# A fused retention and bilinear feed-forward kernel: the opening's four steps in another order, with loads, casts, clears and one PSUM place moved

## The chip, the cores and the metric

The kernel runs on one core of one Trainium2 chip. The metric is the device time of one execution in microseconds; 335.1 us is the median of four runs of the kernel before (334.6 to 335.91). The profile is of one execution, the one that took 335.91 us.

In the profile, PE is TensorE (PEld its weight loads), DVE is VectorE, ACT is ScalarE, POOL is GpSimd and SP is SyncE, which here only issues DMAs. A trailing q, as in SPq or POOLq, is that engine's queue, where DMAs are issued.

## What is computed

A retention layer (attention with a decay in place of the softmax) and a bilinear feed-forward layer on its output, with 8 batches, 8 heads, 576 positions, a head width of 64, a model width of 512 and a feed-forward width of 1536:

```python
scores = scale * np.matmul(q, k.transpose(0, 1, 3, 2))
gamma = 1.0 - 2.0 ** (-5.0 - np.arange(H))
Dmat = np.where(rel >= 0, gamma[:, None, None] ** rel, 0.0)   # rel = row - column
attn = np.matmul(scores * Dmat, v)
x = attn.transpose(0, 2, 1, 3).reshape(B * S, H * D)          # 4608 x 512
out = ((x @ w_a) * (x @ w_b)) @ w_out                         # 4608 x 512
```

Inputs and output are fp32; the kernel multiplies in bf16 and sums in fp32.

## The kernel before, in words

**Retention without the full matrix.** The decay is split into a factor for the key, put on V (tables `vs`), and a factor for the query, put on the result (tables `qs`). Rows are taken in blocks. Within a block the kernel makes scores, masks the upper triangle, and multiplies by V; what earlier rows contribute comes from a state, the sum of outer products of K and V over those rows.

**The opening (lines 143 to 413 and 836 to 895).** The first 512 rows of batch 0 are done in four steps, `STEPS = [(0, 0), (1, 0), (0, 1), (1, 1)]`: step i is (n, hh), the 256 rows from 256 n and the heads from 4 hh. So steps 0 and 1 hold the first four heads, steps 2 and 3 the last four, and steps 1 and 3 need the sum over the rows of steps 0 and 2. For each step there are

- three loads of 256 KB each, Q, K and V (`load_step`, L154, on SP's queue, in an order written out by hand),
- casts of Q and K to bf16 on an engine named in the call (`cast_step`, L315: DVE, POOL or ACT), and V times its decay in two halves `kp` (`values_step`, L319),
- `transpose_step`: four PE transposes (L328) into one PSUM buffer, and a copy to SBUF (L330) on an engine named in the call,
- `score_step`: 16 small matmuls (L343) into the scores' PSUM tile of two banks (pool `ps_sc`, one buffer), and one masked product on DVE (L351) into `sT`, with `mask_s` that POOL makes at the start (L180 to L182),
- `state_step`: 16 or 32 matmuls (L371) of K and V, and two ACT copies (L380) of the result into the diagonal blocks of `state_after`, whose other blocks must be zero (the clear at L262, with that of `two_states`),
- `output_step`: matmuls from the state (L395) and from `sT` and V (L404) into a PSUM tile `o` of two banks (pool `ps_step`, one buffer), and a product with the table `qs` on DVE (L411) into `x`, the feed-forward input. The tables `qs` of the opening are four ACT instructions (`make_qs`, L224) that need an index cast by DVE (L220).

The order of all of these on each engine is the order of the calls at L841 to L895; nothing reorders it. Before, scores and states run in the order 0, 2, 1, 3 and 0, 1, 2, 3, and outputs in the order 0, 1, 2, 3. Between them stand calls `warm(count, n)` (L836): matmuls of a tile of ones whose result nobody reads, which fill PE while it would wait.

**Weights.** `load_w` (L266, L268) and `load_wo` (L271) issue the weight DMAs from POOL's queue, so they start where POOL's program has come to: the columns of the first three of twelve feed-forward tiles of `w_a` and `w_b` among the opening's steps, the others at its end. One later DMA on SP's queue, `gate` (L901), reads from the loaded `w_out`, so that SP's next loads start only when that has landed.

**Feed-forward.** `ffn_begin(F)` (L754) for F in 0, 1, 2 does the first two of the four contractions (`c` 0 and 1, the first four heads) of three tiles of `x @ w_a`, before the others' input exists. `ffn_block` then does, per block of 512 or 256 rows, the other matmuls with `w_a` (L772), with `w_b` (L787), the product of the two (L792), and `w_out` (L807). All three share the PSUM pool `ps_ffn` of four buffers with the transposes, the states and the warm matmuls. The rest of the retention is fed in between these matmuls at due times of a list (`todo`), in units of matmuls. Of these, the prediction speaks of the fifth and sixth 128-row parts of the old form (`one_by_one`, with DVE's cast at L428 and ACT's at L426) and of the POOL casts for later pairs (L555).

Of the kernel before, what the change touches and what calls it, by code (L numbers as in the profile page):

```python
# [10 lines left out]
FP32 = mybir.dt.float32  # L11
# [7 lines left out]
def kernel(  # L19
# [139 lines left out]

    STEPS = [(0, 0), (1, 0), (0, 1), (1, 1)]  # L160
    Q, K, V = 0, 1, 2
    for i, which in ((0, Q), (0, K), (2, K), (2, Q), (1, Q), (0, V),
                     (1, K), (1, V), (3, K), (3, Q), (2, V), (3, V)):
        load_step(*STEPS[i], which)


# [33 lines left out]

    ones = const.tile([128, 512], BF16)
    nc.vector.memset(ones, 1.0)  # L202
    lgp = const.tile([128, HP], FP32)
    for c in range(HP):
        nc.vector.memset(lgp[0:64, c:c + 1], math.log(gammas[2 * c]))
        nc.vector.memset(lgp[64:128, c:c + 1], math.log(gammas[2 * c + 1]))
    biasq = const.tile([128, 1], FP32)
    nc.vector.memset(biasq, math.log(scale))
    idxp_f = const.tile([128, 6], FP32)
    nc.vector.tensor_copy(idxp_f, idxp_i)  # L210
    nc.vector.tensor_scalar_add(idxp_f[64:128, 4:5], idxp_f[64:128, 4:5],
                                -float(S))
    vs = const.tile([128, H, 6], FP32)
    for h in range(H):
        nc.scalar.activation(vs[:, h, :], idxp_f, AF.Exp,
# [7 lines left out]
    def make_qs(c, s0, s1):  # L223
        nc.scalar.activation(qs[:, c, s0:s1], idx_f[:, s0:s1], AF.Exp,  # L224
                             bias=biasq[:, 0:1], scale=lgp[:, c:c + 1])
# [33 lines left out]
    states = [two_states[:, i] for i in (0, 1)]  # L259
    state_after = const.tile([128, 2, 2, HP, 128], BF16)  # L260
    for t in (state_after, two_states):
        nc.vector.memset(t, 0.0)  # L262

    def load_w(f0, f1, which="ab"):
        if "a" in which:
            nc.gpsimd.dma_start(wa_sb[:, :, f0:f1], wa_r[:, :, f0:f1])  # L266
        if "b" in which:
            nc.gpsimd.dma_start(wb_sb[:, :, f0:f1], wb_r[:, :, f0:f1])  # L268
# [45 lines left out]
    def cast_step(i, w, on):  # L314
        COPY[on](by_parity(natural[STEPS[i]][0][:, w]), given(i, w))  # L315

    def values_step(i, kp, on):
        n, hh = STEPS[i]
        on.tensor_tensor(  # L319
            by_parity(natural[n, hh][1])[:, :, kp], given(i, 2)[:, :, kp],  # L320
            vs[:, 4 * hh:4 * hh + 4, 2 * n + kp].unsqueeze(2)
            .to_broadcast([128, 4, D]), op=ALU.mult)

    def transpose_step(i, w, on):
        qkb, qkT = natural[STEPS[i]][0], transposed[STEPS[i]]
        tp = ps_ffn.tile([128, 4, 128], BF16, tag="ab", name="tp")
        for c in range(4):
            nc.tensor.transpose(tp[:, c, :], qkb[:, w, c * 128:c * 128 + 128],  # L328
                                identity)
        COPY[on](qkT[:, w], tp.rearrange("p c x -> p (c x)"))  # L330
# [5 lines left out]
    def score_step(i):  # L336
        key = STEPS[i]
        sc = ps_sc.tile([128, 2, 2, 2, 128], FP32, tag="sc", name="sc0")
        for j in (0, 1):
            for kp in (0, 1):  # L340
                for r, a in QUADS:
                    k0 = kp * 256 + j * 128 + a * 64
                    nc.tensor.matmul(  # L343
                        sc[half(a), r, j, kp],
                        transposed[key][half(r), 1, k0:k0 + 64],
                        queries(key, half(r), j, a),
                        start=(j == 0 and kp == 0), stop=True,
                        skip_group_check=True)
        sT = st_pool.tile([128, 2, 2, 2, 128], BF16, tag="sT", name="sT0")
        scored[key] = sT  # L350
        nc.vector.tensor_tensor(  # L351
            sT.rearrange("p r j k s -> p (r j) (k s)"),
            sc.rearrange("p r j k s -> p (r j) (k s)"),
            mask_s.rearrange("p k q s -> p (k q s)").unsqueeze(1)
            .to_broadcast([128, 4, 256]), op=ALU.mult)

    def state_step(i, behinds):

        n, hh = STEPS[i]
        kv = ps_ffn.tile([128, 2, 2, 64], FP32, tag="ab", name="kv0")  # L360
        fresh = {0, 1}
        for behind in behinds:
            parts = [(0, slice(0, 128))] if n else []
            parts.append((n, slice(0, 128) if behind else half(0)))
            for m, rows in parts:
                qkb, vb = natural[m, hh]
                for j in (0, 1):
                    for kp in (0, 1):
                        for r in (0, 1):
                            e0 = kp * 256 + (2 * j + r) * 64  # L370
                            nc.tensor.matmul(  # L371
                                kv[half(r), behind, j, :],
                                qkb[rows, 1, e0:e0 + 64],
                                vb[rows, e0:e0 + 64],
                                start=r in fresh, stop=True,
                                skip_group_check=True)
                            fresh.discard(r)
        which = slice(behinds[0], behinds[-1] + 1)
        for r in (0, 1):
            nc.scalar.copy(  # L380
                state_after[half(r), n, which, 2 * hh:2 * hh + 2, half(r)],
                kv[half(r), which])

    def output_step(i):
        n, hh = STEPS[i]
        vb = natural[n, hh][1]
        sT = scored.pop((n, hh))
        o = ps_o[0].tile([128, 2, 512], FP32, tag="o", name="o0")
        for a in (0, 1):
            if (n, a) == (0, 0):  # L390
                continue
            st = state_after[:, 0, 0] if (n, a) == (0, 1) else (
                state_after[:, n - 1 + a, 1 - a])
            for j in (0, 1):
                nc.tensor.matmul(o[:, a, 128 * j:128 * j + 128],  # L395
                                 st[:, 2 * hh + j, :],
                                 queries((n, hh), slice(0, 128), j, a),
                                 start=(j == 0), stop=True,
                                 skip_group_check=True)
        for j in (0, 1):  # L400
            for kp in (0, 1):
                for a, r in QUADS:
                    e0 = kp * 256 + (2 * j + r) * 64
                    nc.tensor.matmul(  # L404
                        o[half(r), a, 128 * j:128 * j + 128],
                        vb[half(a), e0:e0 + 64],
                        sT[half(a), r, j, kp],
                        start=((n, a, j, kp) == (0, 0, 0, 0)), stop=True,
                        skip_group_check=True)
        cs = slice(2 * hh, 2 * hh + 2)  # L410
        nc.vector.tensor_tensor(  # L411
            x_of(256 * n, 256)[:, cs].rearrange("p j (a s) -> p a j s", a=2),
            o[:, :, 0:256].rearrange("p a (j s) -> p a j s", j=2),
            qs[:, cs, 256 * n:256 * n + 256]
            .rearrange("p j (a s) -> p a j s", a=2), op=ALU.mult)
# [416 lines left out]
    def warm(count, n):  # L832

        w = ps_ffn.tile([128, 512], FP32, tag="ab", name="w")
        for _ in range(count):
            nc.tensor.matmul(w[:, 0:n], ones[:, 0:128], ones[:, 0:n],  # L836
                             start=True, stop=True)
# [1 line left out]
    W1, W2 = 128 * WCOLS[0], 128 * (WCOLS[0] + WCOLS[1])  # L839
    vector, pool_ = nc.vector, nc.gpsimd  # L840
    warm(8, 512)  # L841
    for c in range(HP):
        make_qs(c, 0, 512)
    for i in range(4):
        place_step(i)
    cast_step(0, Q, "dve")
    cast_step(0, K, "dve")
    transpose_step(0, Q, "dve")
    cast_step(2, K, "pool")
    transpose_step(0, K, "act")  # L850
    warm(4, 256)
    score_step(0)
    transpose_step(2, K, "act")
    warm(4, 256)
    cast_step(1, Q, "act")
    cast_step(2, Q, "pool")
    transpose_step(2, Q, "act")
    warm(4, 256)
    transpose_step(1, Q, "dve")
    values_step(0, 0, pool_)  # L860
    values_step(0, 1, vector)
    warm(2, 256)
    score_step(2)
    cast_step(1, K, "act")
    state_step(0, (0, 1))
    warm(4, 256)
    transpose_step(1, K, "act")
    load_w(0, W1, "a")
    values_step(1, 0, vector)
    warm(3, 256)  # L870
    output_step(0)
    values_step(1, 1, pool_)
    load_w(0, W1, "b")
    score_step(1)
    cast_step(3, K, "act")
    state_step(1, (0,))
    transpose_step(3, K, "act")
    cast_step(3, Q, "pool")
    warm(4, 256)
    transpose_step(3, Q, "act")  # L880
    values_step(2, 0, vector)
    values_step(2, 1, pool_)
    output_step(1)
    state_step(2, (0, 1))
    score_step(3)
    values_step(3, 1, pool_)
    warm(4, 256)
    output_step(2)
    values_step(3, 0, pool_)
    load_w(W1, W2)  # L890
    state_step(3, (0,))
    for F in range(3):
        ffn_begin(F)
    output_step(3)
    warm(3, 256)  # L895
    load_w(W2, DFF)
    for i in (0, 1, 2):
        load_wo(i)
# [100 lines left out]
```

## Time and profile before

| | |
|---|---|
| median of four runs | 335.1 us |
| lowest, highest | 334.6, 335.91 us |
| the profiled execution's own time | 335.91 us |
| its span, first to last instruction | 334.2 us |
| PE busy | 324.9 us, 97% |
| DVE, ACT, POOL busy | 166.8, 128.1, 113.6 us |
| HBM read, written | 37.75 MB, 9.44 MB |
| first matmul of `ffn_block` (L772) | 20.88 us |

The page gives the busy time of each engine, the span in 40 slices of 8.4 us (the tenths of each slice that an engine was busy, and the clock granted to TensorE), and groups of instructions by line with what ended the idle time ahead of them. The timeline lists instructions in order of time: start, length, engine, line, operation, output and inputs, count, and in brackets the idle time before it and what ended that. A row with a count is several instructions of one kind. Starts and lengths can overlap the row before on the same engine a little. The list of waits names the waiting line, its releaser, the total in us, how often, and the longest.

### The profile page before, as it was taken

Reading aid. Unit: us, or ns where it says so; the run is one execution under the profiler, and the core shown is the slowest. Engines: PE = TensorE matmul, PEld = TensorE weight load, DVE = VectorE, ACT = ScalarE, POOL = GpSimd, SP = SyncE. Lnnn points to the kernel's source line nnn. Section 1 sums busy time; section 2 is a strip of 40 time slices with the busy share of each in tenths; the row PEclk is TensorE's granted clock in tenths of the full one; section 3 lists DMA queues with packets and bytes.
Section 4 is the critical chain, followed back from the end, with each engine's and each line's share of the span. In section 5 each row is a group of like instructions: output and inputs, shape, how many; then the busy total and the mean of one; then the engine's idle time right before and its main releaser. Section 6 shows DMA issues by size and latency. Waiting matters only on the chain.

```text
span 334.2 us, 8646 instructions
## 1 busy us (share of the span) xinstructions
PE 324.9 (97%) x3616; PEld 167.6 (50%) x3616; DVE 166.8 (50%) x305; ACT 128.1 (38%) x270; POOL 113.6 (34%) x146
## 2 busy tenths in 40 slices
PE   6999998999999999999999999999999999999996
PEld 2744445857744454545454545454545454444443
DVE  6746337465746465476237623753475347413321
ACT  6734842443624343253225232523342335213321
POOL 4690028760547467267035602470240000000000
PEclk9999999999999999999999999999999999999999
DMA  7999999999999999997599449954970420020002
GB/s 209 233 170 205 208 207 208 230 198 185 179 207 236 216 213 237 191 216 121 148 213 202 66 141 190 212 93 129 198 116 3 125 67 0 3 94 31 2 31 94
DMA packets 146151, 50.37 MB, mean 151 GB/s; under 512 B 130624, under 2 KB 141632, under 8 KB 146112
## 3 DMA queue, kind: packets, MB, share of 16 engines
q1 hardware_dynamic: 141360, 45.10, 66.4%
q0 software_dynamic: 4752, 4.72, 8.9%
q8 instruction: 28, 0.46, 0.6%
q14 instruction: 11, 0.09, 0.1%
HBM read 37.75 MB, written 9.44 MB: 141 GB/s over the span
## 4 chain that ended last, share of the span: by engine, by line
PE 93%; DVE 2%; DMA 2%; ACT 1%; issue 1%; SPq 0%; POOL 0%; ACTq 0%; DVEq 0%; POOLq 0%
PE pa L772 28%; PE pb L787 28%; PE po L807 27%; DMA kf<-in_k_dram 2%; PE o L692 2%; PE o L705 1%; PE sc L666 1%; PE kv L615 1%; PE w L836 1%; PE kv L371 1%; PE tp L328 1%; PE o L404 0%; PE pa L754 0%; DVE xT L532 0%; DVE sT L498 0%
## 5 line engine op out<-in xcount | busy, mean ns | idle before, releaser
L792 DVE TENSOR_TENSOR hT<-ha,pb 128x512 bf16<-128x512 bf16 (+1 forms) x120 | 75.8, 633 | 97.9 <-PE pb L787 85.4
L780 ACT CAST ha<-pa 128x512 bf16<-128x512 f32 (+1 forms) x120 | 64.7, 542 | 123.4 <-PE pa L772 122.7
L787 PE MATMUL pb<-xT,wb_sb 128*128 128x512 bf16 (+1 forms) x480 | 111.8, 358 | 0.1
L772 PE MATMUL pa<-xT,wa_sb 128*128 128x512 bf16 (+1 forms) x474 | 110.3, 358 | 1.1 <-DVE xT L532 0.6
L807 PE MATMUL po<-wo_sb,hT 128*128 128x512 bf16 (+1 forms) x444 | 97.3, 374 | 0.0
L787 PEld LDWEIGHTS <-wb_sb 128*128 128x128 bf16 x480 | 46.7, 98 | 47.3 <-issue 1.1
L772 PEld LDWEIGHTS <-wa_sb 128*128 128x128 bf16 x474 | 45.3, 98 | 46.9 <-issue 2.4
L807 PEld LDWEIGHTS <-hT 128*128 128x128 bf16 x444 | 42.4, 98 | 47.0
L555 POOL CAST qkb<-qf 64x1024 bf16<-64x1024 f32 x15 | 15.4, 1030 | 85.4 <-DMA qf<-in_q_dram 78.0
L818 DVE COPY osb<-po 128x512 f32<-128x512 f32 (+1 forms) x18 | 12.2, 676 | 44.7 <-PE po L807 44.7
L560 POOL TENSOR_TENSOR vb<-vf,vs 128x1024 bf16<-128x1024 f32 x15 | 28.5, 1901 | 8.1 <-DMA vf<-in_v_dram 3.4
L816 ACT COPY osb<-po 128x512 f32<-128x512 f32 (+1 forms) x19 | 10.9, 574 | 45.3 <-PE po L807 45.3
L714 DVE TENSOR_TENSOR xT<-o,qs 128x512 bf16<-128x512 f32 x30 | 19.6, 681 | 5.3 <-PE o L705 5.3
L634 DVE TENSOR_TENSOR sums<-kv,sums 128x256 f32<-128x256 f32 x47 | 19.8, 422 | 4.6 <-PE kv L615 3.1
L675 DVE TENSOR_TENSOR sT<-sc,mask 128x512 bf16<-128x512 f32 x30 | 19.7, 679 | 0.0
L559 POOL CAST qkb<-qf 64x512 bf16<-64x512 f32 x30 | 17.7, 617 | 1.9 <-DMA qf<-in_q_dram 1.3
L559 POOL CAST qkb<-kf 64x512 bf16<-64x512 f32 x30 | 17.6, 614 | 0.9
L555 POOL CAST qkb<-kf 64x1024 bf16<-64x1024 f32 x15 | 15.5, 1033 | 7.0 <-DMA kf<-in_k_dram 6.7
L646 ACT CAST states<-sums 64x512 bf16<-64x512 f32 (+1 forms) x30 | 17.2, 574 | 0.5
L836 PE MATMUL w<-ones 128*128 128x256 bf16 (+1 forms) x40 | 8.4, 340 | 1.5 <-DVE ones L202 1.5
L431 POOL TENSOR_TENSOR vb<-vf,vs 128x512 bf16<-128x512 f32 x2 | 2.1, 1057 | 22.1 <-DMA vf<-in_v_dram 22.1
L224 ACT ACTIVATE qs<-qs,biasq,lgp 128x384 f32<-128x384 f32 (+1 forms) x12 | 8.0, 734 | 2.4 <-DVE qs L247 2.4
(103 smaller groups left out, 159.2 us busy)
## 6 DMA issues: line engine op xcount, KB each, us to landing
qf<-in_q_dram SPq DMA_DIRECT2D x32, 256.0 KB, 4.5
kf<-in_k_dram SPq DMA_DIRECT2D x32, 256.0 KB, 5.2
vf<-in_v_dram SPq DMA_DIRECT2D x32, 256.0 KB, 5.3
out_dram<-osb SPq DMA_DIRECT2D x31, 256.0 KB, 2.2
wo_sb<-in_moe_w_out_dram POOLq DMA_DIRECT2D x3, 512.0 KB, 16.6
out_dram<-osb SPq DMA_DIRECT2D x10, 128.0 KB, 2.6
qf<-in_q_dram SPq DMA_DIRECT2D x8, 128.0 KB, 4.8
kf<-in_k_dram SPq DMA_DIRECT2D x8, 128.0 KB, 5.4
```

The lines of the kernel that those rows point to most:

```text
L555: nc.gpsimd.tensor_copy(qkb[0:64, w], t[0:64])
L559: nc.gpsimd.tensor_copy(to[:, :, 1 - r], fro[:, :, r])
L560: nc.gpsimd.tensor_tensor(vb.rearrange("p (k h d) -> p k h d", k=2, h=H), vf.rearrange("p (k h d) -> p k h d", k=2, h=H), vs2[:, n % BL].u ...
L634: nc.vector.tensor_tensor(sums[:, i], own, prev, op=ALU.add)
L646: nc.scalar.copy(into[half(1 - r)].rearrange("p (k a) c d -> p a k (c d)", a=2)[:, 1, which.start // 2: which.stop // 2], sums[half(r)].re ...
L675: nc.vector.tensor_tensor(sT[:, on].rearrange("p c k s -> p (c k) s"), sc[:, on].rearrange("p c k s -> p (c k) s"), mask3.unsqueeze(1).to_ ...
L714: nc.vector.tensor_tensor(x_of(t0, 128).rearrange("p c (a s) -> p c a s", a=2), o[:, :, :, kp].rearrange("p a c s -> p c a s"), qs[:, :, s ...
L772: nc.tensor.matmul(pa[:, 0:n], wa_sb[:, c, fs], xT[:, c], start=(c == 0), stop=(c == NC - 1))
L780: nc.scalar.copy(ha[:, 0:n], pa[:, 0:n])
L787: nc.tensor.matmul(pb[:, 0:n], wb_sb[:, c, fs], xT[:, c], start=(c == 0), stop=(c == NC - 1))
L792: nc.vector.tensor_tensor(hT[:, F, 0:n], has[F][:, 0:n], pb[:, 0:n], op=ALU.mult)
L807: nc.tensor.matmul(po[:, 0:width], hT[:, F, u * 128:(u + 1) * 128], wo_sb[:, F, cols], start=(F == 0), stop=(F == NF - 1))
```

## The change

It does the following.

- Loads: step 1's K and Q come third and fourth, then V of step 0, then step 2's three, K and Q of step 3, V of step 1 and V of step 3. The count, the sizes and the queue stay.
- The calls of the opening are put in another order: scores 0, 1, 2, 3; states 0, 2, 1, 3; outputs 0, 2, 1, 3. Output 1 and output 3 follow step 3's state, and the three `ffn_begin` follow both. Casts, values and copies get other engines: step 0's Q is copied by ACT and its K by DVE; step 1's K and Q are cast by POOL and copied by DVE; step 2's K is cast by POOL and copied by ACT, its Q cast by ACT and copied by DVE; step 3's K and Q are cast by POOL, copied by ACT and DVE. V of steps 0 and 3 is scaled by POOL, of step 2 by DVE, of step 1 by one of each.
- The warm matmuls between score 0 and step 3's state are 35 of 256 columns in place of 25; the three after output 3 are gone.
- `output_step(3, ps_sc)` puts the last output into the scores' two PSUM banks in place of `o`.
- Two of the four opening `make_qs` calls stand behind ACT's copy of step 0's Q.
- The index cast for `vs` stands ahead of the small DVE memsets.
- The clears of `state_after` and `two_states` are POOL memsets in place of DVE ones; in POOL's program they stand behind the making of `mask_s` and ahead of its first cast.
- The first `w_a` and `w_b` DMAs are issued behind POOL's cast of step 2's K, one behind the other.

```diff
-    for i, which in ((0, Q), (0, K), (2, K), (2, Q), (1, Q), (0, V),
-                     (1, K), (1, V), (3, K), (3, Q), (2, V), (3, V)):
+    for i, which in ((0, Q), (0, K), (1, K), (1, Q), (0, V), (2, Q),
+                     (2, K), (2, V), (3, K), (3, Q), (1, V), (3, V)):
         load_step(*STEPS[i], which)
...
     ones = const.tile([128, 512], BF16)
     nc.vector.memset(ones, 1.0)
+    idxp_f = const.tile([128, 6], FP32)
+    nc.vector.tensor_copy(idxp_f, idxp_i)
+    nc.vector.tensor_scalar_add(idxp_f[64:128, 4:5], idxp_f[64:128, 4:5],
+                                -float(S))
     lgp = const.tile([128, HP], FP32)
...
-    idxp_f = const.tile([128, 6], FP32)
-    nc.vector.tensor_copy(idxp_f, idxp_i)
-    nc.vector.tensor_scalar_add(idxp_f[64:128, 4:5], idxp_f[64:128, 4:5],
-                                -float(S))
...
     for t in (state_after, two_states):
-        nc.vector.memset(t, 0.0)
+        nc.gpsimd.memset(t, 0.0)
...
-    def output_step(i):
+    def output_step(i, place=None):
...
-        o = ps_o[0].tile([128, 2, 512], FP32, tag="o", name="o0")
+        if place is None:
+            o = ps_o[0].tile([128, 2, 512], FP32, tag="o", name="o0")
+        else:
+            o = place.tile([128, 2, 512], FP32, tag="sc", name="o0")
...
     warm(8, 512)
-    for c in range(HP):
-        make_qs(c, 0, 512)
+    make_qs(0, 0, 512)
+    make_qs(1, 0, 512)
     for i in range(4):
         place_step(i)
     cast_step(0, Q, "dve")
     cast_step(0, K, "dve")
-    transpose_step(0, Q, "dve")
-    cast_step(2, K, "pool")
-    transpose_step(0, K, "act")
+    transpose_step(0, Q, "act")
+    transpose_step(0, K, "dve")
+    cast_step(1, K, "pool")
+    cast_step(1, Q, "pool")
+    make_qs(2, 0, 512)
+    make_qs(3, 0, 512)
     warm(4, 256)
     score_step(0)
-    transpose_step(2, K, "act")
-    warm(4, 256)
-    cast_step(1, Q, "act")
-    cast_step(2, Q, "pool")
-    transpose_step(2, Q, "act")
+    for kp in (0, 1):
+        values_step(0, kp, pool_)
+    cast_step(2, K, "pool")
+    warm(6, 256)
+    transpose_step(1, K, "dve")
     warm(4, 256)
     transpose_step(1, Q, "dve")
-    values_step(0, 0, pool_)
-    values_step(0, 1, vector)
+    warm(5, 256)
+    score_step(1)
+    cast_step(2, Q, "act")
+    warm(2, 256)
+    state_step(0, (0, 1))
+    transpose_step(2, Q, "dve")
+    load_w(0, W1, "a")
+    for kp in (0, 1):
+        values_step(2, kp, vector)
+    warm(4, 256)
+    transpose_step(2, K, "act")
+    output_step(0)
+    load_w(0, W1, "b")
     warm(2, 256)
     score_step(2)
-    cast_step(1, K, "act")
-    state_step(0, (0, 1))
-    warm(4, 256)
-    transpose_step(1, K, "act")
-    load_w(0, W1, "a")
-    values_step(1, 0, vector)
-    warm(3, 256)
-    output_step(0)
-    values_step(1, 1, pool_)
-    load_w(0, W1, "b")
-    score_step(1)
-    cast_step(3, K, "act")
+    state_step(2, (0, 1))
+    cast_step(3, K, "pool")
+    cast_step(3, Q, "pool")
+    warm(5, 256)
+    transpose_step(3, K, "act")
+    values_step(1, 0, pool_)
+    values_step(1, 1, vector)
+    warm(2, 256)
+    transpose_step(3, Q, "dve")
+    output_step(2)
     state_step(1, (0,))
-    transpose_step(3, K, "act")
-    cast_step(3, Q, "pool")
-    warm(4, 256)
-    transpose_step(3, Q, "act")
-    values_step(2, 0, vector)
-    values_step(2, 1, pool_)
+    for kp in (0, 1):
+        values_step(3, kp, pool_)
+    load_w(W1, W2)
+    score_step(3)
+    warm(5, 256)
+    state_step(3, (0,))
     output_step(1)
-    state_step(2, (0, 1))
-    score_step(3)
-    values_step(3, 1, pool_)
-    warm(4, 256)
-    output_step(2)
-    values_step(3, 0, pool_)
-    load_w(W1, W2)
-    state_step(3, (0,))
+    output_step(3, ps_sc)
     for F in range(3):
         ffn_begin(F)
-    output_step(3)
-    warm(3, 256)
     load_w(W2, DFF)
```

## The prediction

> **What bounds the kernel now.** I read the page first, then the waits of TensorE (PE) in the first 22 us, then the timeline of the opening.
>
> ```profile
> span 334.2 us, 8646 instructions
> PE 324.9 (97%) x3616; PEld 167.6 (50%) x3616; DVE 166.8 (50%) x305; ACT 128.1 (38%) x270; POOL 113.6 (34%) x146
> PE   6999998999999999999999999999999999999996
> PEclk9999999999999999999999999999999999999999
> ```
>
> PE is busy 97% of the span, at an undiminished granted clock. Only 9.3 us are idle, most of them in the first slice. The change touches only what is issued before the feed-forward part (FFN), which starts at 20.88 us; from there the same instructions stand in the same order on all engines. So the whole effect is the time at which the FFN's first full matmul (L772) starts, plus what a shifted PE meets later.
>
> The waits of PE in that stage (us in total, times, longest):
>
> ```profile
> PE sc L343 <- ACT qkT L330: 0.7, 1, 0.7
> PE tp L328 <- POOL qkb L315: 0.5, 1, 0.5
> PE pa L772 <- DVE xT L411: 0.4, 1, 0.4
> ```
>
> Removable waits are small, since "warm" matmuls fill the rest. The timeline at the end of the opening (start, length, engine):
>
> ```profile
> 15.86 1.20 POOL L319 TENSOR_TENSOR vb<-vf,vs 128x256 bf16<-128x256 f32 x2 [0.80 <-DMA vf<-in_v_dram]
> ...
> 17.45 0.56 PE L371 MATMUL kv<-vb,qkb 128*64 128x64 bf16 x16
> ...
> 18.04 1.47 PE L754 MATMUL pa<-xT,wa_sb 128*128 128x512 bf16 x6
> ...
> 20.13 0.69 DVE L411 TENSOR_TENSOR xT<-o,qs 128x512 bf16<-128x512 f32 x1 [1.81 <-PE o L404]
> ...
> 20.88 1.45 PE L772 MATMUL pa<-xT,wa_sb 128*128 128x512 bf16 x6 [0.36 <-DVE xT L411]
> ```
>
> The last V lands at 15.8, GpSimd (POOL) scales it until 17.06, and PE starts step 3's state at 17.45, 0.35 us after it could. Two things thus bound the opening almost equally: the twelve loads, and PE's own queue.
>
> **The loads.** By issue and time to landing, positions 1 to 12 land at 3.7, 4.5, 7.3, 8.2, 9.0, 10.0, 10.8, 11.8, 12.7, 13.5, 14.3, 15.8. Same queue, sizes and count after: the new order only renames them (V of step 0 at 9.0 in place of 10.0; V of step 3 still last). The first weight DMA moves on POOL behind the cast of the seventh load: from 10.68 to about 11.5. It took 7.3 us to land, so 18.0 becomes at most 18.9. Its user, the early FFN matmuls, starts at 19.1 or later (below): hidden by 0.2 us, and up to 0.3 if the transfer is slower. Competing later, it may let the last load land up to 0.4 earlier, which I don't count.
>
> **Start of the opening.** Here is the part that matters most:
>
> ```profile
> 2.61 0.97 POOL L182 TENSOR_SCALAR_AFFINE_SELECT mask_s<-mask_s 64x256 bf16<-64x256 bf16 x2
> ...
> 3.47 0.91 DVE L262 MEMSET state_after<- 128x1024 uint32 x1 [0.16 <-issue]
> ...
> 4.44 0.48 DVE L262 MEMSET state<- 128x512 uint32 x1
> 4.85 0.36 DVE L315 CAST qkb<-qf 128x512 bf16<-128x512 f32 x1
> 5.13 0.41 DVE L315 CAST qkb<-kf 128x512 bf16<-128x512 f32 x1
> ...
> 7.16 0.42 PE L343 MATMUL sc<-qkT 64*64 64x128 bf16 x16 [0.73 <-ACT qkT L330]
> ```
>
> Removed: 1.39 us of memsets on VectorE (DVE), ahead of casts whose data landed at 3.7 and 4.5, and two of the four query tables (0.77 each) on ScalarE (ACT) ahead of the copy that the first score waits for. If nothing else acted: DVE casts end at 4.1 and 4.9, PE transposes behind its 3.4 us of warming until 5.7, ACT (tables done by 4.95) and DVE copy until about 6.2, score 0 at 6.3: 0.85 earlier. Moving the index cast ahead of the small memsets only feeds ACT earlier; ACT then waits for DVE's cast at 2.79 to 3.32 anyway: nothing.
>
> But the memsets go to POOL, behind the masks, from 3.58. After the change they are 128x2048 and 128x1024 bf16 elements, not half as many uint32. POOL's memsets of 128 and 256 elements took 0.214 and 0.311: 0.76 ns an element, so 1.67 + 0.89 = 2.6 us (until 6.2); scaling the 0.311 row whole gives 2.5 + 1.2 = 3.7 (until 7.3). I take 2.6, as the slope leaves the fixed cost out. The Trainium skill's VectorE: DVE Perf Modes (Zero memsets can be issued as uint32) says a DVE memset costs a cycle per element; by the DVE rows (0.91 for 1024) the clears would be 1.39.
>
> Does that matter? In this trace a cast on DVE waits for POOL:
>
> ```profile
> 42.68 0.43 DVE L428 CAST qkb<-kf 128x512 bf16<-128x512 f32 x1 [0.47 <-DMA kf<-in_k_dram]
> ...
> 50.49 1.03 POOL L555 CAST qkb<-qf 64x1024 bf16<-64x1024 f32 x1 [1.38 <-DMA qf<-in_q_dram]
> ...
> 50.71 1.10 DVE L428 CAST qkb<-kf 128x512 bf16<-128x512 f32 x1
> ```
>
> The same cast takes 0.43 alone and 1.10 beside a POOL cast, ending 0.3 after it. The Trainium skill's SBUF — State Buffer (Who interferes with whom) gives the rule: a DVE copy or cast in a two-port mode and a GpSimd instruction exclude each other for a whole instruction. The rows show it against a POOL cast; that a memset, which only writes, does it too is the page's claim, and speaks against this change. By the rows read narrowly score 0 is at 6.3; by the rule: memset 3.58 to 5.25, Q cast to 5.65, second memset to 6.5, K cast to 6.95, transposes to 7.35, DVE copy to 7.85, score 0 at 7.9, 0.7 later than before. If both casts slip in before the second memset, 6.9. I take the rule, 7.9.
>
> **PE between score 0 and step 3's state.** Before: 17.45 - 7.16 = 10.3 us, of which 0.85 waits (0.48 ahead of the first transpose, 0.33 ahead of step 0's state): 9.4 of work. After: warm matmuls 35 in place of 25, at 0.11 (0.44 for four): +1.1; output 1 moves behind: -0.6. So 9.9. From 7.9 that is 17.8; from 6.3 or 6.9 the last load decides (17.1).
>
> Side changes lie beside this. Casts and copies move off ACT (three copies of 0.56 and two casts of 0.62 fewer), to POOL (two casts more, 1.2, within its waits for loads of 1.3 and more) and DVE (three copies of 0.42 more, 1.3). DVE's copies of step 1's K and Q now queue behind mask 0 (1.22): from score 0 at 7.9, mask to 9.5, copies to 10.4, when PE with its 17 warm matmuls reaches score 1 at 10.6. Hidden by 0.2; if that cover fails, the same shows one for one. Both values of step 0 on POOL: V at 9.0, done 10.4, needed at 11. Steps 2 and 3 have one more load's time each.
>
> **Behind step 3's state.** Before: 0.56 state, 1.47 early FFN, 0.60 output 3, 0.70 DVE and 0.1 of latencies: 3.43 to L772. After: state 0.56, output 1 0.6, its DVE product 0.75 (output 3 beside it on PE, in the scores' banks; in the old banks it would wait for this product, about 0.7), early FFN 1.47, under which output 3's product (0.69) lies: 3.4. The early FFN now waits for output 1's product, behind it on PE wait all later matmuls; the wait replaces the one for output 3's. So nothing is won: 0.05. The three warms at the end filled a wait.
>
> **Sum.** L772 at 17.8 + 3.4 = 21.2 in place of 20.88: +0.3. At 50.5 to 51.8 a later PE (up to 0.6) only shortens the DVE cast's wait for POOL, whose end is set by a load: some of the 0.3 vanishes. A PE over 0.22 earlier would start that cast ahead of POOL (50.71 against 50.49) and win the 0.67 too, if the load lands the same. The profiled run has span 334.2 and time 335.91, 1.7 outside; it is the slowest of four, 0.8 over the median 335.1. I put the change on the median: +0.2, 335.3, which a measurement of this kernel (0.3%, 1.0 us) can't tell from no change.
>
> **Rivals.**
> A (forecast): the lock eats what leaving DVE wins, 335.3. Chance 0.43.
> B, faster: memsets don't hold off the casts, or both slip in. State 3 starts at 17.1, L772 at 20.5 (-0.4); the collision at 50.5 is avoided (-0.67): 334.0. For it: nothing in the trace shows a memset blocking. Against: 17.1 is the floor of the loads, and the collision may be peculiar to the profiled run. 0.22.
> C, slower: POOL's memsets at the dear end hold both casts until 7.3; casts to 8.0, transposes and copy to 8.9, score 0 at 8.95, state 3 at 18.85, L772 at 22.25 (+1.4): 336.5. It decides from the point at which score 0 starts after 7.5, since PE's queue (9.9) then has no idle time to give back. For it: the 1.10 row, and that this PE queue holds 1.1 us more filler. Against: the 0.76 ns slope. 0.27.
> D: the change doesn't do what it says, as the last load and PE's queue rule: 335.1. 0.08.
>
> Range: B's 334.0 to a little past C, as a wait I don't see inside the new order shows one for one: 334.0 to 336.9. Faster 0.22; within 0.3% (A, D less a little) 0.46; slower 0.32.
>
> **What would show it.** In the profile after: POOL's two L262 memsets, 1.7 and 0.9 long from 3.6; DVE's casts of step 0 longer than 0.41 or starting after 5.2 (A), or ended by 4.9 (B); score 0 at 7.9 (6.3 in B, 9 in C); step 3's state at 17.8, with PE without waits before it; L772 at 21.2; the cast at 50.7 still over 0.43. I am wrong if PE waits over 0.5 us for weights at L757, if the granted clock drops while PE idles at 5 to 8 us, or if the FFN's later stages differ with an equal start.

## The result, and the profile after

| | before | after |
|---|---|---|
| median (lowest to highest), first series | 334.69 us (334.26 to 336.87), 55 executions | 336.6 us (334.19 to 338.35), 34 |
| ratio, with 95% interval | | 1.004 [1.0027, 1.0054] |
| the same kernel, second series | 334.8 us | 335.0 us (334.1 to 337.69), 22 |
| ratio, with 95% interval | | 1.0013 [0.9999, 1.0026] |
| profiled execution: time, span | 335.91, 334.2 us | 335.12, 333.4 us |
| first full feed-forward matmul, L772 (after: L775) | 20.88 us | 19.94 us |

The two kernels do not only differ in their medians. Of the first series of after, 13 executions lie at 334.2 to 335.4 us and 21 at 336.2 to 338.4; nearly all of before lie at 334.2 to 335.9. The profiled execution of after is one of the short ones. Its page, span, busy time and the 40 slices:

```profile
span 333.4 us, 8661 instructions
PE 325.1 (98%) x3623; PEld 168.3 (50%) x3623; DVE 167.2 (50%) x306; ACT 125.7 (38%) x265; POOL 118.0 (35%) x150
PE   6999999999999999999999999999999999999996
PEclk9999999999999999999999999999999999999999
```

PE is as full as before; POOL has 4.4 us more, 3.3 of them the two clears. Two of PE's waits (line and releaser; total, times, longest):

```profile
PE tp L328 <- DVE qkb L315: 0.9, 1, 0.9
PE sc L669 <- DMA qkT<-qkb: 0.7, 1, 0.7
```

The first is in the opening; the second, at 137 us, is one that the profile of before does not have. The start of the opening, timeline of after (start, length):

```profile
3.74 0.43 DVE L315 CAST qkb<-qf 128x512 bf16<-128x512 f32 x1 [0.26 <-DMA qf<-in_q_dram]
3.82 2.09 POOL L262 MEMSET state_after<- 128x2048 bf16 x1
4.57 1.62 DVE L315 CAST qkb<-kf 128x512 bf16<-128x512 f32 x1 [0.40 <-DMA kf<-in_k_dram]
...
5.85 1.23 POOL L262 MEMSET state<- 128x1024 bf16 x1
...
6.48 0.60 PE L839 MATMUL w<-ones 128*128 128x256 bf16 x4
...
7.16 0.42 PE L343 MATMUL sc<-qkT 64*64 64x128 bf16 x16
```

Q's cast starts 0.08 us ahead of the first clear and takes its usual 0.43. The cast of K starts inside the clear, lasts 1.62 in place of 0.41 to 0.43, and ends 0.28 after it. Score 0 is at 7.16, just where it was before. The end of the opening:

```profile
14.99 1.20 POOL L319 TENSOR_TENSOR vb<-vf,vs 128x256 bf16<-128x256 f32 x2 [0.61 <-DMA vf<-in_v_dram]
...
16.61 0.56 PE L371 MATMUL kv<-vb,qkb 128*64 128x64 bf16 x16
...
18.64 1.45 PE L757 MATMUL pa<-xT,wa_sb 128*128 128x512 bf16 x6
...
19.94 1.46 PE L775 MATMUL pa<-xT,wa_sb 128*128 128x512 bf16 x6
```

Step 3's state starts 0.84 earlier than in the profile of before, the feed-forward part 0.94. PE did not wait for weights at L757. At 50 us DVE's cast now comes ahead of POOL's and is short:

```profile
49.77 0.42 DVE L431 CAST qkb<-kf 128x512 bf16<-128x512 f32 x1
51.51 1.03 POOL L558 CAST qkb<-qf 64x1024 bf16<-64x1024 f32 x1 [1.93 <-DMA qf<-in_q_dram]
```

By that profile the change wins 0.8 us; by the medians it loses 0.2 to 1.9. One profile is one execution, and here the executions differ. Two questions follow: what makes the long ones, and what of the short one's lead is the change's.

### The profile page after: what moved, and what is told of

It reads as the page before. It is cut to its first block, busy times and chain, and to the rows that moved or that the text cites. A ratio compares the mean times of both kernels' runs of the same rounds, so it can differ in the third digit from the quotient of the medians.

```text
span 333.4 us, 8661 instructions
## 1 busy us (share of the span) xinstructions
PE 325.1 (98%) x3623; PEld 168.3 (50%) x3623; DVE 167.2 (50%) x306; ACT 125.7 (38%) x265; POOL 118.0 (35%) x150
## 4 chain that ended last, share of the span: by engine, by line
PE 58%; SPq 17%; DMA 17%; POOL 6%; issue 1%; ACT 0%; POOLq 0%
PE po L810 19%; PE pa L775 18%; PE pb L790 18%; SPq L143 10%; DMA kf<-in_k_dram 5%; DMA wo_sb<-in_moe_w_out_dram 5%; DMA vf<-in_v_dram 3%; SPq L154 2%; SPq L127 2%; DMA qf<-in_q_dram 2%; POOL vb L563 2%; POOL qkb L562 2%; SPq L589 2%; DMA qkT<-qkb 1%; POOL qkb L558 1%
## 5 line engine op out<-in xcount | busy, mean ns | idle before, releaser
L775 PE MATMUL pa<-xT,wa_sb 128*128 128x512 bf16 (+1 forms) x474 | 110.3, 358 | 0.8 <-DVE xT L535 0.6
L775 PEld LDWEIGHTS <-wa_sb 128*128 128x128 bf16 x474 | 45.4, 98 | 46.6 <-issue 1.9
L839 PE MATMUL w<-ones 128*128 128x256 bf16 (+1 forms) x47 | 9.5, 334 | 1.5 <-DVE ones L202 1.5
```

Source lines behind the costliest of these rows:

```text
L775: nc.tensor.matmul(pa[:, 0:n], wa_sb[:, c, fs], xT[:, c], start=(c == 0), stop=(c == NC - 1))
```

## The experiments

Line numbers shift by a few between the kernels. "The start" is the first full feed-forward matmul.

### 1. The same kernel again

> The changed kernel as it is, for more profiles and for the clock and span of each execution. Theory L (loads): the opening ends about 0.9 us earlier and TensorE then runs into the load chain (POOL casts, DMA transposes), so dear executions show TensorE waiting 1 to 4 us for a DMA or a POOL cast behind 60 us, at a mean clock of 1.0. Theory C (clock): TensorE has too little to do between 5 and 7 us, while the K cast waits for POOL's memset, and in some executions the clock is halved [...]; those have a mean clock of 0.995 and are 1.7 us longer, and the drop lies in the first 10 us. Both: a median of 335 to 337 us, with a spread of 334.2 to 338.4.

Edit: none. 335.0 us, ratio 1.0013 [0.9999, 1.0026]; 18 executions at 334.1 to 335.7, 4 at 336.8 to 337.7. The profiled one took 336.92, a long one. Its opening:

```profile
3.81 2.10 DVE L315 CAST qkb<-qf 128x512 bf16<-128x512 f32 x1 [0.32 <-DMA qf<-in_q_dram]
3.83 1.80 POOL L262 MEMSET state_after<- 128x2048 bf16 x1
...
5.57 1.23 POOL L262 MEMSET state<- 128x1024 bf16 x1
5.83 1.25 DVE L315 CAST qkb<-kf 128x512 bf16<-128x512 f32 x1
...
7.54 1.06 PE L839 MATMUL w<-ones 128*128 128x256 bf16 x4
...
8.53 0.64 PE L343 MATMUL sc<-qkT 64*64 64x128 bf16 x16
```

Q landed 0.07 later, and that turned the order around. The clear is now the undelayed one (1.80 against 2.09), and Q's cast, which the record starts 0.02 ahead of it, is blocked to 5.91, 0.28 after the clear. PE is idle from 5.12 to 5.97, and until 10.3 its matmuls run at half rate: four warm ones start 0.21 apart in place of 0.11 and take 1.06 in all in place of 0.60, and the score takes 0.64 in place of 0.42. The page's clock row stays all nines, which the last section explains. The start is at 22.09, 2.15 later than in the other profile: K's cast ends 0.89 later (7.08 against 6.19), transposes, copy and warm matmuls add 0.48, and from score 0 to step 3's state PE needs 10.24 in place of 9.45, 0.79 more.

So the change holds a race, two starts whose order is settled anew in each execution: Q lands at 3.7 to 3.8, and POOL is done with the mask at 3.82.

### 2. The clears back on DVE, the rest of the change kept

```diff
-        nc.gpsimd.memset(t, 0.0)
+        nc.vector.memset(t, 0.0)
```

> The changed kernel with the two clears back on DVE (1.4 us ahead of the casts of step 0), nothing else. Theory C: the K cast is no longer 1.6 long, TensorE has its transposes earlier or about as early (5.2 to 5.9) and the executions with a mean clock of 0.995 are gone; the median falls by 1 us or more. Theory L: score 0 within 0.3 us of the changed kernel's, L775 at 19.9, the same dear executions at a clock of 1.0, median unchanged within 0.7 us.

334.8 us, ratio 1.0004 [0.9987, 1.0021]. The clears take 0.91 and 0.48 from 3.65, the casts 0.36 and 0.41 behind them, score 0 is at 6.99, the start at 20.01, the profiled time 335.18. It is level with before. The second series of the change itself, 1.0013, can't be told from this; that the clears make it slower rests on its first series and on the next experiment.

### 3. Before, with only the clears on POOL

```diff
-        nc.vector.memset(t, 0.0)
+        nc.gpsimd.memset(t, 0.0)
```

> The kernel before with only the two clears on POOL. Theory C: executions with a mean clock of 0.995 appear in it too, median 0.5 to 1.7 us above the kernel before. Theory L: nothing is gained at the end of the opening (it waits for loads), so no change: within 0.5 us, clock 1.0. The prediction's lock: one of the casts of step 0 is longer than 1 us.

336.28 us, ratio 1.0036 [1.0024, 1.0049]. The clears alone cost what the whole change cost in its first series. Eight of the 22 executions have a mean granted clock of 0.995; the median of the other 14 is 335.75, still 0.95 above before. In this order POOL reaches them 0.2 earlier and wins against the cast in the profile:

```profile
3.64 1.80 POOL L262 MEMSET state_after<- 128x2048 bf16 x1
3.71 2.01 DVE L315 CAST qkb<-qf 128x512 bf16<-128x512 f32 x1 [0.40 <-DMA qf<-in_q_dram]
5.38 1.23 POOL L262 MEMSET state<- 128x1024 bf16 x1
5.64 1.25 DVE L315 CAST qkb<-kf 128x512 bf16<-128x512 f32 x1
```

Score 0 is at 8.02 and the start at 21.24 (time 335.49). PE, idle from 5.12 to 5.78, was back at full rate by 7.18 here (four warm matmuls 0.60).

### 4. A later start of the feed-forward part

```diff
         ffn_begin(F)
+    warm(9, 256)
     load_w(W2, DFF)
```

> The changed kernel with nine more warm matmuls between the early feed-forward matmuls and the first full one, so that this starts near 20.9 as in the kernel before; loads, POOL and DVE keep the new order. Theory L: TensorE no longer runs ahead of the load chain, the dear executions at a clock of 1.0 go, median 334.7 to 335.3. Theory C: the opening's clock drops stay, a third of the executions at 0.995, median 336.5 to 337.5. A third theory W (the new order itself delays the weights and so all later loads): dear executions at a clock of 1.0 stay, with less waiting each.

335.95 us, ratio 1.0029 [1.0017, 1.004]: six executions at 335.4 to 336.2, two at 337.6 and 338.0. About 1 us of warm matmuls costs about 1 us. The profiled execution (338.0) is one in which the clear won; its start is at 23.19, against 22.09. So a short start is not given back behind, and the long executions are not made by TensorE running ahead of its later loads.

### 5. The clears behind the casts

```diff
-    for t in (state_after, two_states):
-        nc.gpsimd.memset(t, 0.0)
...
     cast_step(0, K, "dve")
+    nc.vector.memset(state_after, 0.0)
...
     make_masks()
+    nc.gpsimd.memset(two_states, 0.0)
```

> The changed kernel with the clear of state_after on DVE behind step 0's K cast (0.91 of uint32) and that of two_states on POOL behind the last masks; so neither stands ahead of, or beside, the casts. Theory P (the port): POOL's first memset and DVE's Q cast start within 0.1 us of each other at 3.8, and whichever is first holds the other off; without that race the casts end at 4.1 and 5.0, score 0 starts at 6.4 to 6.6, L775 at 19.6 to 19.9, hardly any execution over 336.2, median 333.9 to 334.5. Theory L (TensorE ahead of the loads loses again what it wins): the same L775, but the median stays at 334.7 or above, as with the clears ahead of the casts.

334.72 us, ratio 0.9991 [0.9979, 1.0003], all between 333.5 and 336.1. The first casts meet no clear any more:

```profile
3.75 0.43 DVE L313 CAST qkb<-qf 128x512 bf16<-128x512 f32 x1 [0.26 <-DMA qf<-in_q_dram]
4.62 0.43 DVE L313 CAST qkb<-kf 128x512 bf16<-128x512 f32 x1 [0.44 <-DMA kf<-in_k_dram]
5.21 0.91 DVE L849 MEMSET state_after<- 128x1024 uint32 x1 [0.16 <-issue]
6.45 0.42 PE L341 MATMUL sc<-qkT 64*64 64x128 bf16 x16 [0.18 <-DVE qkT L328]
```

Score 0 is at 6.45, step 3's state at 15.84, the start at 19.18, the time 333.52. The long executions are gone: with experiment 12, none of 35 is above 336.1, against 25 of the 56 of after in its two series.

### 6. The clears on POOL, but a little later

```diff
+    nc.gpsimd.memset(mask, 1.0)
+    nc.gpsimd.memset(mask, 1.0)
     for t in (state_after, two_states):
         nc.gpsimd.memset(t, 0.0)
```

> The changed kernel with two small POOL memsets (128x128, about 0.2 us each, rewritten later) ahead of the two clears, so that these start at about 4.2 and not at 3.8; POOL has more work, not less. Theory P: DVE's Q cast always starts first, so every execution is like the good ones of the changed kernel: K cast still about 1.6 long, score 0 at 7.2 to 7.7, L775 at 20 to 20.4, few or no executions over 336.2, median 334.7 to 335.3. Without theory P: 0.4 us more on POOL can't help, a third to two thirds of the executions stay at 336.2 to 338.4.

336.02 us, ratio 1.0036 [1.002, 1.0051]. The race is decided as meant, for the cast, and the spread closes: 335.0 to 337.0, but for one at 339.9 whose mean clock is 0.995. Yet the median is no better:

```profile
3.78 0.53 DVE L317 CAST qkb<-qf 128x512 bf16<-128x512 f32 x1 [0.29 <-DMA qf<-in_q_dram]
...
4.40 1.80 POOL L264 MEMSET state_after<- 128x2048 bf16 x1
4.64 1.83 DVE L317 CAST qkb<-kf 128x512 bf16<-128x512 f32 x1 [0.33 <-DMA kf<-in_k_dram]
...
6.15 1.22 POOL L264 MEMSET state<- 128x1024 bf16 x1
```

With Q's cast safe, K's is blocked for 1.4; POOL's own casts of step 1 queue behind the second clear, to 7.43 in place of 6.50 (experiment 5). Score 0 is at 7.45, 1.00 later than in experiment 5, and the start at 20.71, 1.53 later. So the clears on POOL cost in both outcomes of the race, only less in one. Of the 0.53 behind score 0, 0.30 is a second collision of the same two engines: PE waits for step 2's V, whose two multiplies on DVE take 1.77 beside POOL's casts of step 3, in place of 0.75 in the profile of after.

### 7. PE kept busy over the blocked cast

```diff
-    warm(8, 512)
+    warm(12, 512)
```

> The changed kernel with 12 opening warm matmuls of 512 columns in place of 8, so that TensorE is busy to about 6 us. Theory C2: in the dear executions half of the loss is that TensorE, idle from 5.1 to 6, goes on at half rate until 10.3 (1.06 for four warm matmuls in place of 0.6, 1.4 for six in place of 0.83: 1.5 us in all). With it: dear executions fall to 335 to 336.8, those with transposes early may lose up to 0.8; in the profile, if the Q cast is over 1.5 long, four warm matmuls still take about 0.6. If only the port matters: dear executions stay at 336.5 to 338.4, and four warm matmuls take about 1 us.

335.92 us, ratio 1.0024 [1.0012, 1.0036], 334.6 to 336.8. In the profile the cast was first and the four warm matmuls behind took 0.60. No execution is above 336.8, where the unedited kernel reached 337.7 and 338.4. But PE, held by its own warm matmuls, now starts the transposes only at 6.63. Score 0 is at 8.15, and behind it PE waits 0.57 for step 2's V (its two multiplies take 2.19 beside POOL's casts), so the start is at 21.83 and the short executions are lost. It fits that idle PE makes the longest ones; it doesn't prove it. No profile has the clear first with PE busy, and PE was idle for 0.66 in experiment 3, 0.92 in the profile of after and 0.98 in experiment 6, and yet at full rate in the warm matmuls behind.

### 8. The last output in the old banks

To experiment 2:

```diff
-    output_step(3, ps_sc)
+    output_step(3)
```

> The changed kernel with the clears on DVE and output 3 in the old banks, so that it waits for output 1's DVE product. By the prediction's step the wait is 0.7 on TensorE ahead of output 3, so the early matmuls and L775 start about 0.65 later than with the scores' banks (20.0 with the clears on DVE): 20.6 to 20.7.

One execution, 335.05 us. PE waits where the prediction had put it, and the start is at 20.69 against 20.01, 0.68 later. Score 0 was 0.27 later too, but step 3's state (16.69, against 16.68) no longer was:

```profile
PE o L398 <- DVE xT L414: 0.8, 1, 0.8
```

### 9 and 10. Before, unchanged, profiled twice more

> The kernel before, unchanged, profiled a second time: a control on its one profile, in which the FFN's first full matmul (L772) started at 20.88, the last V was ready to be scaled at 15.86 (in every profile of a version of the new kernel at 13.4 to 15.2), and a DVE cast ran beside a POOL cast at 50.7. If that profile is typical (the reading so far), L772 is at 20.7 to 21.0 again, and the time minus that start 314.4 to 315.1. If the late V was chance, V is scaled from about 14.9, step 3's state starts 0.3 to 0.6 earlier, L772 is at 20.3 to 20.6, and the new order's lead at that point is that much smaller than the two profiles say. PE's queue (9.4 us of work behind score 0 at 7.16, two short waits) allows no more than that.

> The kernel before, unchanged, profiled a third time, for the spread of what the second shows: score 0 at 7.1 to 7.2 in each (no race: its clears are on DVE itself, in program order with the casts), L772 between 20.3 and 21.0, and a time that follows it but for up to 0.7 us, which depends on whether DVE's cast near 50 us comes before POOL's.

334.7 and 334.37 us. Both starts are 0.85 earlier than in the first profile (lines of the first of the two):

```profile
7.15 0.42 PE L343 MATMUL sc<-qkT 64*64 64x128 bf16 x16
...
14.53 1.21 POOL L319 TENSOR_TENSOR vb<-vf,vs 128x256 bf16<-128x256 f32 x2 [0.17 <-DMA vf<-in_v_dram]
...
16.71 0.56 PE L371 MATMUL kv<-vb,qkb 128*64 128x64 bf16 x16
...
20.03 1.46 PE L772 MATMUL pa<-xT,wa_sb 128*128 128x512 bf16 x6 [0.36 <-DVE xT L411]
```

This is a correction to the reading of before and of everything since. Score 0 stands, but the third and fourth loads' casts and the last V came 0.8 to 1.3 later in the first profile; that was the chance of one execution. Without it step 3's state is at 16.71, and behind score 0 there is only 0.2 of waits. Against 20.03, the change's short execution (19.94) leads by 0.09, not by 0.94, and its long one (22.09) is 2.06 behind. In the second of the two, DVE's cast at 49.86 took 0.41: the collision at 50 us isn't in every execution of before either.

### 11. Before, with the clears behind the casts

The edit of experiment 5, made to the kernel before.

> The kernel before, old order, with only the clears behind the first two casts: state_after's on DVE after step 0's K cast, two_states' on POOL behind the opening's masks. DVE's casts of step 0 then start when their loads land, at 3.7 and 4.5, about 1.1 and 0.6 earlier than before. Theory T (ACT's four query tables are the second gate, so leaving DVE alone wins nothing): score 0 still at 7.0 to 7.2, since ACT's copy of K stands behind four tables until 6.6; L772 at 20.4 to 20.9, the time 334.6 to 334.9, ratio 0.999 to 1.001. Rival U (the clears were the only gate, and the order adds nothing): score 0 at 6.4 to 6.6, L772 0.5 to 0.7 earlier, the time 334.2, ratio 0.998.

334.51 us, ratio 1.0003 [0.9981, 1.0026]. The casts move up to 3.73 and 4.60, and nothing follows from it:

```profile
6.54 0.56 ACT L328 COPY qkT<-tp 128x512 bf16<-128x512 bf16 x1
...
7.15 0.42 PE L341 MATMUL sc<-qkT 64*64 64x128 bf16 x16 [0.88 <-ACT qkT L328]
```

ACT's copy stands behind its four query tables until 6.54, and PE waits 0.88 for it; the start is at 20.03, as before to the hundredth. Freeing DVE is worth 0.7 at score 0 (6.45 against 7.15) only together with what the change does on ACT: two tables behind its copy, and Q's copy on it in place of K's. These two were not run apart.

### 12. Experiment 5 once more

> The changed kernel with the clears behind the first casts, the best version so far (334.72, ratio 0.9991 [0.9979, 1.0003]), once more with a new profile. If its profile (score 0 at 6.45, L775's counterpart L773 at 19.18, 1.7 us ahead of the profile before) is typical, and the start passes through one for one, the median should be 1 us or more under the kernel before: 333.7, ratio 0.997. If the start is early but not all of it reaches the end in most executions, the profile shows L773 at 19.2 again, and the ratio is 0.999 to 1.0 as in the first run; then what the later part takes back shows as PE waits or collisions behind 20 us in executions that end at 335 rather than 333.5.

334.95 us, ratio 0.9999 [0.9988, 1.0011]; the profiled execution took 335.18. Score 0 and step 3's state start as early as they did in experiment 5, but here the last V came late, as it had in the first profile of before:

```profile
15.80 0.32 PE L369 MATMUL kv<-vb,qkb 128*64 128x64 bf16 x8
15.87 1.20 POOL L317 TENSOR_TENSOR vb<-vf,vs 128x256 bf16<-128x256 f32 x2 [1.74 <-DMA vf<-in_v_dram]
16.54 0.22 PE L369 MATMUL kv<-vb,qkb 64*64 64x64 bf16 x2 [0.43 <-POOL vb L317]
17.12 0.28 PE L369 MATMUL kv<-vb,qkb 64*64 64x64 bf16 x6 [0.36 <-POOL vb L317]
```

PE waits 0.8 for it, the start is at 20.17, and at 137 us there is 0.5 of the wait that the profile of after has. The best order found is thus held by the loads: where they come early in both kernels it gains 0.85 at the start (19.18 against 20.03). Where the last V comes late in both (15.87, and 15.86 in the first profile of before), it gains 0.71 (20.17 against 20.88), though in that profile of before two earlier loads were late too; a late V against an early one leaves nothing.

The place of the clear isn't free either. PE has transposed K by 5.44, and DVE copies it only behind the clear; score 0 waits for this copy:

```profile
5.14 0.91 DVE L849 MEMSET state_after<- 128x1024 uint32 x1 [0.16 <-issue]
5.97 0.36 DVE L328 COPY qkT<-tp 128x512 bf16<-128x512 bf16 x1
6.38 0.26 PEld L341 LDWEIGHTS <-qkT 64*64 64x64 bf16 x16 [0.79 <-DVE qkT L328]
```

That is up to 0.5 at score 0 here (in experiment 5, with the transposes until 5.84, under 0.2). ACT first writes into the cleared tile at 10.2, so the clear could stand behind the copy; that was not run.

With the clear behind the casts the kernel is the fastest of all versions in single executions (333.52), and in the median not shown to be faster than before.

## Why the prediction was right or wrong, point by point

The number (335.3, range 334.0 to 336.9) lies between the two medians of after, 335.0 and 336.6, and the range holds both; the first series puts the sign on "slower", to which I gave 0.32. That the number fits is in part luck, as the forecast describes an execution that no profile shows: score 0 lies at 7.16 or at 8.53, and was forecast at 7.9.

**The lock: right in kind, wrong as one course of events.** The prediction took the rule of the Trainium skill, SBUF — State Buffer (Who interferes with whom), over the rows. The rows now show it for a memset: a cast of 0.43 lasts 1.57 to 2.10 when the first POOL clear is under way, 1.25 with the second, and ends 0.27 to 0.28 after it, in every profile with such clears. The page also says that the order of issue decides who blocks; the step that failed is to have fixed that order ("memset 3.58 to 5.25, Q cast to 5.65"). It took the end of the mask, 3.58, from the old order; in the new one the mask's two last passes took 1.15 in place of 0.97, for a reason that no run shows, and the clear started at 3.82. With Q's cast at 3.74 the two were within 0.1 us, and the two profiles show each order once. Rival B's half of it (Q's cast first) and rival C's (both held) are both executions of the one kernel. That the long executions are those in which the clear wins rests on two profiled ones (336.92 in experiment 1, 338.0 in experiment 4, both at a mean clock of 0.999 or more), and on the closed spread of experiments 5 and 6. It is not shown for all: ten of the 21 long ones of the first series have a mean clock of 0.994 to 0.995, which would by itself cost some 1.7 us (an estimate, 0.005 of 335). Less that they would lie at 334.9 to 336.1, half of them among the short ones (up to 335.4). None of them has a profile, so for these the order of the race stays open, and so does what lowered the clock.

**The clears: slightly mis-sized.** 1.80 and 1.23, 3.03 in sum, in place of 2.6. The 1.23 reads as 0.94, what the same clear took alone at 22.5 us in experiment 5, and 0.28 for the cast that slips in between the two clears. So the choice of the slope over the dear end (3.7) was right, and 2.74 of own work is near 2.6. I left out what experiment 6 shows: POOL's casts of step 1 wait behind the clears.

**PE between score 0 and step 3's state.** Forecast 9.9, measured 9.45 (and 9.39, 9.41 in experiments 5 and 12), so this term was 0.45 too dear. Its base, 9.4 of "work", was 10.3 less listed waits only; in the control the whole stretch is 9.56, and two gaps of 0.26 and 0.18 ahead of a transpose and a state lie within. The work of before is then 9.1, and 9.1 + 1.1 − 0.7 (output 1) is 9.5. With the clear first it is 10.24, at the half rate that I had named only as a way to be wrong.

**The loads: wrong.** "Positions 1 to 12 land at" took one execution for the rule, with 15.8 for the last, and a floor of 17.1 for step 3's state. In twelve of the thirteen later profiles POOL began on the last V by 15.15, and step 3's state started as early as 15.84 (experiment 5). This is why the forecast saw +0.3 against 20.88 where the comparison should have been with 20.03. Two errors offset: a start forecast 1.3 too late for the short execution (21.2, measured 19.94), and a base 0.85 too late. Against 20.03 the forecast's own 21.2 would have been +1.2, and by the controls' 334.37 and 334.7 the time 335.6 to 335.9 (an estimate).

**Behind step 3's state: right.** 3.4 forecast, 3.33 measured; the bank's 0.7, measured 0.68. **Weights: right**, no wait at L757.

**What a shifted PE meets later: right, and a second one beside it.** In the profiles the time less the start, less the one wait behind it that differs, is 314.25 to 314.51 (before: 335.91 − 20.88 − 0.7 = 314.33; after: 335.12 − 19.94 − 0.7 = 314.48; experiment 1: 336.92 − 22.09 − 0.5 = 314.33), but for experiment 6 with 314.75, whose 0.2 to 0.5 more I can't place. So the start passes through one for one, and a wait of 0 to 0.7 comes on top: for DVE's cast beside POOL's at 50 us or, in the profile of after and experiment 12, for the transfer at 137 us. The change in the profile avoids the first and meets the second. An early start doesn't by itself bring the second: experiment 5, with the earliest (19.18), has neither.

**Where the gain went.** Moving the clears, two tables and a copy off the path is worth 0.7 at score 0 (experiment 5). With the clears on POOL it is gone where the cast wins (score 0 at 7.16, against 7.15), and the start is 2.1 later where it loses (22.09, against 20.03). What stays open is why the share of long executions was 21 of 34 in the first series and 4 of 22 in the second. Of these, 10 and 1 had the lower clock. The second series ran on the chip numbered 0, and the chip of the first isn't known, so a difference of chips isn't ruled out.

## What to carry to other kernels

Work moved from VectorE to GpSimd to free VectorE's queue isn't off VectorE's path while casts run there: look at what the two would do in the same microsecond, and put such work where neither has a deadline. Behind the casts was better here, and behind the copy that follows them might be better still. Where two starts lie within 0.1 us of each other, forecast both orders, and say that the kernel will have both. Profile the kernel before more than once: its first profile had loads that were up to 1.3 us late, and every comparison made from it was off by 0.85 us.

## What the runs showed of the hardware

- **A memset on GpSimd holds off a VectorE cast whole**, and the reverse holds too: 2.03 to 2.09 for the clear that came second, 1.80 for the one that came first.
- **VectorE's multiplies of V** collide with GpSimd's casts too: two of 128x256 took 0.75 alone, and 1.53, 1.77 and 2.19 in experiments 2, 6 and 7, where POOL cast K and Q of step 3 meanwhile.
- **GpSimd's memset** took 1.80 us for 128x2048 bf16 and 1.22 to 1.23 for 128x1024 directly behind it, but 0.94 for the same 128x1024 alone at 22.5 us (experiment 5). In each profile with the longer ones a DVE cast ended 0.32 to 0.34 after their start, so the memset seems to have waited for the cast; no run separates that from a cost of standing behind another memset.
- **TensorE at half rate with the clock row at nine**: four warm matmuls took 1.06 in experiments 1, 4 and 8, 0.98 in experiment 9, 0.60 to 0.69 in the other profiles, always within the first 10.3 us. The clock grants stored in each trace go with it: the first, of the full clock, starts at 10.30 in experiment 1 and at 10.13 in 4, and between 4.41 and 7.44 in the other profiles (7.38 in 8, 6.85 in 9). The page's row and the mean clock, 0.999 and more in the profiled executions, count the time ahead of that first grant as full, so they don't tell of it. The Trainium skill, TensorE: Matmul & The Clock Gate (Part 1, What's actually happening), has a window of about 3.4 us that runs freely, so that the switch to full rate varies by execution; the runs agree in that experiments 2 and 8, with the same instructions at the same times until 6.27, differ (0.69 and 1.06), and so do experiments 9 and 10, the same kernel (0.98 and 0.65). One such window earlier than measured, the full clock would have come at 6.9 and 6.7 in experiments 1 and 4 (an estimate), just behind PE's idle 0.85; in experiments 3 and 6 it came at 6.09 and 6.06, in the midst of the idle time. That fits idle PE as what held it back, but two profiles don't prove it.
- **A lower mean clock**, 0.994 to 0.995, was recorded for 10 of the 34 executions in the first series of after and 8 of 22 in experiment 3, both with early POOL clears, and for at most one in each of the other series. In experiment 3 their median is 336.87, that of the others 335.75. I have no profile of such an execution.
